# Two products of a chunked delta-rule attention as 32x32 array tiles

## The chip, the core and the metric

The kernel runs on one core of one Trainium2 chip. The metric is device time in microseconds (us), from the start to the end of one execution. Two executions of the kernel before took 905.57 and 912.49 us; their median is 909.03 us.

The core's engines run their own queues in order: TensorE (PE in the rows; its weight loads are PEld), VectorE (DVE), ScalarE (ACT), GpSimd (POOL) and SyncE (SP), which issues most transfers.

## The reference

Attention first: for each of 4 sequences and 8 heads a 48x48 state is carried over 768 positions.

```
k_n = k / (norm(k) + 1e-6)
for t in range(S):
    y[t] = q[t] @ state
    v_old = k_n[t] @ state
    state += beta[t] * outer(k_n[t], v[t] - v_old)
```

The outputs, 3072 rows of 384, go to a mixture of 8 experts: each row takes the expert with the largest of `x @ w_gate`, is multiplied by two weight matrices (384x1024, a ReLU, 1024x384), and is scaled by its softmax weight. All is fp32.

## The kernel before

The 768 positions are cut into 24 chunks of 32. One step of the main loop treats one chunk for all 4 sequences at once: partition 32b + i is position i of sequence b, so a 128-row tile holds the four sequences one below the other. "Step c" below is one turn of this loop.

Ahead of a step, `scores(c + 7)` multiplies keys by keys and queries of a chunk into `pa` (L164). ScalarE copies the key part out as `gr` (L173), and VectorE multiplies the query part by a mask that keeps only what lies within one sequence and in causal order: `qk` (L175). `gr` is stored to memory. Every fourth step `solve` loads the four chunks' key products and inverts 128 triangular 32x32 systems in place on VectorE: L249, then 30 pairs of a product (L255) and an addition (L259), then L262. The result is stored, and `fetch_step` loads it as four 32x32 blocks for each head onto the diagonal of a 128x128 tile `ub`, whose other places are zero since the start.

`chain(c)` is the step itself, in this order of dependence:
- `ph` (L291): keys times states, 16 matmuls that load 32 columns each and write to the 32 partitions of one sequence. VectorE takes it from the values: the residual `R` (L296).
- the first part of `pq` (L303): queries times states, of the same shape as `ph`.
- `pz` (L310): the triangular block times the residual, 8 matmuls, one for each head, with all 128x128 of `ub` as weights. ScalarE copies it out as `Z` (L315).
- `pw` (L323): keys times Z, in two halves of 8 matmuls, two sequences each, written to two PSUM banks. VectorE adds it to `states` (L331). The next step's `ph` needs them.
- the second part of `pq` (L335): masked scores times Z, 8 matmuls, one for each head, added onto the first part. ScalarE copies the output out as `xg` (L445).

After every fourth step `route` computes the gate of the last chunks on PE (transposes L349, products L353, counts L389 and L390) and VectorE. `pa` and `pw` share two PSUM buffers (pool `psS`); `ph`, `pq`, `pz` and the routing's tiles share four (pool `psC`). The order of the instructions on each engine is made once, when the program is built, by a scheduler that has its own idea of how long each takes; at run time each queue is worked off in that order. After the 24 steps come the experts (L508 to L555), whose weights are loaded by SP.

Of the kernel before, what the change touches and what calls it, by code (L numbers as in the profile page):

```python
# [19 lines left out]
B, H, S, D = 4, 8, 768, 48  # L20
C = 32
# [43 lines left out]
def kernel(  # L65
# [12 lines left out]
    nc = tc.nc  # L78
# [202 lines left out]
    def chain(c):  # L281
        kq, ub, kt, vt, qk = kqs.pop(c), ubufs[c % NU], kts.pop(c), vts.pop(c), qks.pop(c)
        vtl = vt[:].rearrange("p h d -> p (h d)")
        if c == 0:
            Rv = vtl
        else:
            ph = psC.tile([128, 512], FP32, name="ph", tag="pc")
            for p in range(NP):
                for b in range(B):
                    r = slice(C * b, C * b + C)  # L290
                    nc.tensor.matmul(  # L291
                        ph[r, 96 * p : 96 * p + 96], lhsT=kq[:, p, 0, r],
                        rhs=states[:, b, p, :], start=True, stop=True, skip_group_check=True,
                    )
            R = work.tile([128, DM], FP32, name="R")
            nc.vector.tensor_tensor(out=R[:], in0=vtl, in1=ph[:, 0:DM], op=OP.subtract)  # L296
            Rv = R[:]
        pq = psC.tile([128, 512], FP32, name="pq", tag="pc")
        if c > 0:
            for p in range(NP):  # L300
                for b in range(B):
                    r = slice(C * b, C * b + C)
                    nc.tensor.matmul(  # L303
                        pq[r, 96 * p : 96 * p + 96], lhsT=kq[:, p, 1, r],
                        rhs=states[:, b, p, :],
                        start=(p == 0), stop=False, skip_group_check=True,
                    )
        pz = psC.tile([128, 512], FP32, name="pz", tag="pc")
        for h in range(H):
            nc.tensor.matmul(  # L310
                pz[:, D * h : D * h + D], lhsT=ub[:, h, :], rhs=Rv[:, D * h : D * h + D],
                start=True, stop=True,
            )
        Z = work.tile([128, DM], FP32, name="Z")
        nc.scalar.activation(out=Z[:], in_=pz[:, 0:DM], func=AF.Copy)  # L315
        if c < NS - 1:
            for half in range(2):
                pw = psS.tile([128, 2, 512], FP32, name="pw", tag="ps")
                for p in range(NP):
                    for bb in range(2):  # L320
                        b = 2 * half + bb
                        r = slice(C * b, C * b + C)
                        nc.tensor.matmul(  # L323
                            pw[:, bb, 96 * p : 96 * p + 96], lhsT=kt[r, p, :],
                            rhs=Z[r, 96 * p : 96 * p + 96], start=True, stop=True,
                        )
                pv = pw[:, :, 0:DM].rearrange("q b (p w) -> q b p w", p=NP)
                for e in range(2):
                    r = slice(64 * e, 64 * e + 64)
                    sv = states[r, 2 * half : 2 * half + 2, :, D * e : D * e + D]  # L330
                    nc.vector.tensor_tensor(  # L331
                        out=sv, in0=sv, in1=pv[r, :, :, D * e : D * e + D], op=OP.add
                    )
        for h in range(H):
            nc.tensor.matmul(  # L335
                pq[:, D * h : D * h + D], lhsT=qk[:, h, :], rhs=Z[:, D * h : D * h + D],
                start=(c == 0), stop=True, skip_group_check=True,
            )
        return pq


# [93 lines left out]
    for c in range(NS):  # L435
        load_kq(c + AHEAD + 1)
        scores(c + AHEAD)
        if (c + AHEAD) % GS == GS - 1:
            solve((c + AHEAD) // GS)
            factors((c + AHEAD) // GS + 1)  # L440
        pq = chain(c)
        ss = first[c]
        if c == ss[0]:
            xg = work.tile([128, GS, ROW], FP32, name="xg")
        nc.scalar.activation(out=xg[:, c - ss[0], 0:DM], in_=pq[:, 0:DM], func=AF.Copy)  # L445
        if c in batch:
            route(ss, xg)
        fetch_step(c + 3)
        if c == NS // 2:
            weights[0] = load_w(moe_w1[0], moe_w2[0], wpool)  # L450
# [196 lines left out]
```

## Time and profile before

| | us |
|---|---|
| median of two runs | 909.03 |
| the profiled execution | 910.19 |
| its span, first to last instruction | 908.4 |
| first product of the main loop | 77.81 |
| end of the main loop's part (last routing) | 548.3 |
| experts | 579.9 to 908.4 |

| engine | busy us | share of the span |
|---|---|---|
| PE matmuls | 720.9 | 79% |
| PE weight loads | 526.7 | 58% |
| DVE | 328.1 | 36% |
| ACT | 109.5 | 12% |
| POOL | 158.1 | 17% |

Matmuls are pipelined, so a busy PE is not a PE at its peak, and weight loads overlap with matmuls. The mean granted clock of TensorE is 0.732 of full speed (0.5 is 1.2 GHz, 1.0 is 2.4 GHz).

### The profile page before, as it was taken

To read this page: it belongs to the slowest core of one execution; us is meant where nothing else is said; L and a number is where in the kernel's file an instruction comes from. 1 tells how busy PE (TensorE), PEld (TensorE's weight loads), DVE (VectorE), ACT (ScalarE), POOL (GpSimd) and SP (SyncE) were. 2 spreads that over 40 slices of the span, in tenths; PEclk is the share of its full clock that TensorE was granted. 3 is DMA by queue.
4 is the path that set the end of the run, shared out by engine and by line. 5 is a ranking of instruction groups with operands and counts; after the bars stand their busy time and mean duration, and the time that the engine had idled before them with its cause. 6 is when DMAs were issued, how large, how long until landed. Compare 5 with 4: busy or idle time off the path is not lost. (4 is left out here: it accounts for less than half of the span.)

```text
span 908.4 us, 11550 instructions
## 1 busy us (share of the span) xinstructions
PE 720.9 (79%) x4596; PEld 526.7 (58%) x4597; DVE 328.1 (36%) x897; ACT 109.5 (12%) x199; POOL 158.1 (17%) x133
## 2 busy tenths in 40 slices
PE   4515768879978897599874980399999999999993
PEld 3315658768866786488864970155555555555551
DVE  4592882395458529632552121011011111102100
ACT  2210111201110111011000110001010010101100
POOL 5201211020211112101001011303031231312101
PEclk8655767565655665567555555599999999999997
DMA  8536335631634287335112005501233432323000
GB/s 319 163 78 172 81 90 130 149 92 43 177 98 110 59 182 224 91 97 87 37 56 63 1 27 175 163 0 55 85 104 112 143 121 87 114 95 96 28 8 18
DMA packets 112345, 91.55 MB, mean 101 GB/s; under 512 B 85238, under 2 KB 96678, under 8 KB 112288
## 3 DMA queue, kind: packets, MB, share of 16 engines
q1 hardware_dynamic: 106704, 80.37, 31.7%
q0 software_dynamic: 4608, 9.47, 3.4%
q10 hardware_dynamic: 976, 0.94, 0.4%
q8 instruction: 37, 0.61, 0.3%
q14 instruction: 20, 0.16, 0.1%
HBM read 70.96 MB, written 21.36 MB: 102 GB/s over the span
## 5 line engine op out<-in xcount | busy, mean ns | idle before, releaser
L517 PE MATMUL phe<-xTe,w1t 128*128 128x448 f32 x384 | 148.4, 547 | 0.0
L533 PE MATMUL pye<-w2t,hT 128*128 128x384 f32 x384 | 125.1, 486 | 0.0
L517 PEld LDWEIGHTS phe<-xTe,w1t 128*128 128x128 f32 x384 | 73.1, 192 | 70.1 <-issue 68.2
L164 PE MATMUL pa<-kq 64*128 64x256 f32 x384 | 82.0, 593 | 33.6 <-issue 11.3
L533 PEld LDWEIGHTS pye<-w2t,hT 128*128 128x128 f32 x384 | 73.0, 190 | 51.7 <-issue 3.0
L323 PE MATMUL pw<-Z,kt 32*128 32x96 f32 x736 | 64.4, 366 | 29.5 <-issue 10.1
L164 PEld LDWEIGHTS pa<-kq 64*128 64x128 f32 x384 | 58.0, 302 | 50.0 <-issue 29.3
L310 PE MATMUL pz<-R,ub 128*128 128x48 f32 x368 | 67.5, 356 | 23.4 <-DMA ub<-solved 15.4
L335 PE MATMUL pq<-Z,qk 128*128 128x48 f32 x384 | 78.4, 383 | 6.3 <-ACT Z L315 5.7
L310 PEld LDWEIGHTS pz<-R,ub 128*128 128x128 f32 x368 | 64.3, 271 | 30.0 <-issue 17.0
L323 PEld LDWEIGHTS pw<-Z,kt 32*128 32x128 f32 x736 | 58.2, 265 | 39.9 <-issue 32.7
L335 PEld LDWEIGHTS pq<-Z,qk 128*128 128x128 f32 x384 | 74.5, 297 | 10.3 <-ACT Z L315 8.0
L331 DVE TENSOR_TENSOR states<-states,pw 64x384 f32<-64x384 f32 x92 | 50.7, 552 | 69.6 <-PE pw L323 67.7
L175 DVE TENSOR_TENSOR qk<-pa,cf 128x256 f32<-128x256 f32 x96 | 37.9, 418 | 103.9 <-ACT gr L173 101.9
L255 DVE TENSOR_TENSOR tmp<-u 128x30 f32<-128x30 f32 (+9 forms) x180 | 70.1, 389 | 4.7
L259 DVE TENSOR_TENSOR u<-u,tmp 128x30 f32<-128x30 f32 (+9 forms) x180 | 64.9, 360 | 4.2
L522 DVE TENSOR_SCALAR hT<-phe 128x448 f32<-128x448 f32 x32 | 20.0, 625 | 127.5 <-PE phe L517 127.5
L405 POOL DMA_INDIRECT lists<-ids,ri x24 | 23.9, 996 | 216.8 <-DVE ri L403 89.7
L497 POOL DMA_INDIRECT out_dram<-y,rows x24 | 24.0, 1002 | 211.5 <-ACT y L542 178.1
L291 PE MATMUL ph<-states,kq 128*32 128x96 f32 x736 | 40.6, 361 | 10.2 <-DVE states L331 10.2
L512 DVE COPY xTe<-px 128x448 f32<-128x448 f32 x24 | 14.1, 614 | 89.8 <-PE px L508 89.8
L508 PE MATMUL px<-ident,xin 128*128 128x128 f32 (+1 forms) x96 | 19.0, 303 | 33.7 <-issue 31.6
(87 smaller groups left out, 578.4 us busy)
## 6 DMA issues: line engine op xcount, KB each, us to landing
kq<-in_kq_t_dram SPq DMA_DIRECT2D x24, 512.0 KB
w1t<-in_moe_w_dram SPq DMA_DIRECT2D x8, 1536.0 KB
w2t<-in_moe_w_dram SPq DMA_DIRECT2D x8, 1536.0 KB
kt<-in_k_tok_dram SPq DMA_DIRECT2D x24, 256.0 KB
kb<-in_k_blk_dram SPq DMA_DIRECT2D x6, 768.0 KB
vb<-in_v_blk_dram SPq DMA_DIRECT2D x6, 768.0 KB
sv<-vb SPq DMA_DIRECT2D x6, 768.0 KB
vt<-sv SPq DMA_DIRECT2D x96, 48.0 KB
```

What stands on the lines that cost most here:

```text
L164: nc.tensor.matmul(pa[:, e, pp, :], lhsT=kq[r, 2 * g + pp, 0, :], rhs=kq[r, 2 * g + pp, :, :].rearrange("p j w -> p (j w)"), start=True, s ...
L175: nc.vector.tensor_tensor(out=heads(qk)[:, e], in0=pa[:, e, :, 128:256], in1=blockmask.unsqueeze(1).to_broadcast([128, 2, 128]), op=OP.mult,)
L255: nc.vector.tensor_tensor(out=tv, in0=u[:, 0:j, j].unsqueeze(2).to_broadcast([128, j, w]), in1=u[:, j, j + 1 : C].unsqueeze(1).to_broadcas ...
L259: nc.vector.tensor_tensor(out=u[:, 0:j, j + 1 : C], in0=u[:, 0:j, j + 1 : C], in1=tv, op=OP.add)
L291: nc.tensor.matmul(ph[r, 96 * p : 96 * p + 96], lhsT=kq[:, p, 0, r], rhs=states[:, b, p, :], start=True, stop=True, skip_group_check=True,)
L310: nc.tensor.matmul(pz[:, D * h : D * h + D], lhsT=ub[:, h, :], rhs=Rv[:, D * h : D * h + D], start=True, stop=True,)
L323: nc.tensor.matmul(pw[:, bb, 96 * p : 96 * p + 96], lhsT=kt[r, p, :], rhs=Z[r, 96 * p : 96 * p + 96], start=True, stop=True,)
L331: nc.vector.tensor_tensor(out=sv, in0=sv, in1=pv[r, :, :, D * e : D * e + D], op=OP.add)
L335: nc.tensor.matmul(pq[:, D * h : D * h + D], lhsT=qk[:, h, :], rhs=Z[:, D * h : D * h + D], start=(c == 0), stop=True, skip_group_check=True,)
L497: nc.gpsimd.indirect_dma_start(out=out, out_offset=bass.IndirectOffsetOnAxis(ap=index, axis=0), in_=y[0:w, :], in_offset=None, bounds_chec ...
L517: nc.tensor.matmul(ph[:], lhsT=w1t[:, s, f * 128 : f * 128 + 128], rhs=xT[:, s, :], start=(s == 0), stop=(s == NK - 1),)
L533: nc.tensor.matmul(py[:], lhsT=hT[:, f, t * 128 : t * 128 + w], rhs=w2t[:, f, :], start=(f == 0), stop=(f == NF - 1),)
```

## The change

Both products are issued as 4 matmuls for each head in place of one: each takes one sequence's 32x32 diagonal block as weights and writes to that sequence's 32 partitions. The sums are the same, since the other blocks are zero. The tiles themselves, the zeros around the blocks and the mask are unchanged. The lines below move by two (`pw` from L323 to L325) and then four (`pq` from L335 to L339).

```diff
         for h in range(H):
-            nc.tensor.matmul(
-                pz[:, D * h : D * h + D], lhsT=ub[:, h, :], rhs=Rv[:, D * h : D * h + D],
-                start=True, stop=True,
-            )
+            for b in range(B):
+                r = slice(C * b, C * b + C)
+                nc.tensor.matmul(
+                    pz[r, D * h : D * h + D], lhsT=ub[r, h, r], rhs=Rv[r, D * h : D * h + D],
+                    start=True, stop=True, skip_group_check=True,
+                )
...
         for h in range(H):
-            nc.tensor.matmul(
-                pq[:, D * h : D * h + D], lhsT=qk[:, h, :], rhs=Z[:, D * h : D * h + D],
-                start=(c == 0), stop=True, skip_group_check=True,
-            )
+            for b in range(B):
+                r = slice(C * b, C * b + C)
+                nc.tensor.matmul(
+                    pq[r, D * h : D * h + D], lhsT=qk[r, h, r], rhs=Z[r, D * h : D * h + D],
+                    start=(c == 0), stop=True, skip_group_check=True,
+                )
```

The scheduler orders the program anew. On PE in step 4, from `pz` to the next step's `pz` (the number after `ub_` is a buffer, x32 a count of matmuls), it stood so before:

```order
L310 MATMUL pz<-R,ub_95 128x48 x8
L335 MATMUL pq<-Z,qk 128x48 x8
L164 MATMUL pa<-kq 128x256 x8
L323 MATMUL pw<-Z,kt 128x96 x16
L291 MATMUL ph<-states,kq 32x96 x2
L303 MATMUL pq<-states,kq 32x96 x2
L291 MATMUL ph<-states,kq 32x96 x14
L303 MATMUL pq<-states,kq 32x96 x14
L310 MATMUL pz<-R,ub_97 128x48 x8
```

And so after the change:

```order
L312 MATMUL pz<-R,ub_95 32x48 x32
L164 MATMUL pa<-kq 128x256 x8
L325 MATMUL pw<-Z,kt 128x96 x8
L339 MATMUL pq<-Z,qk 32x48 x5
L325 MATMUL pw<-Z,kt 128x96 x8
L339 MATMUL pq<-Z,qk 32x48 x27
L291 MATMUL ph<-states,kq 32x96 x2
L303 MATMUL pq<-states,kq 32x96
L291 MATMUL ph<-states,kq 32x96 x14
L303 MATMUL pq<-states,kq 32x96 x15
L312 MATMUL pz<-R,ub_97 32x48 x32
```

The second part of `pq` moved from ahead of the scores to behind the first half of `pw`; in steps 7, 11 and 16 it also moved behind `pw` or into it, and `pa` of steps 8 and 12 moved from ahead of `pz` to behind it.

On DVE the residual `R` of step 7 stood before in the midst of the solve of the third group, 26 rows ahead of L262:

```order
L331 TENSOR_TENSOR states<-states,pw 64x8x48
L255 TENSOR_TENSOR tmp<-u 128x228
L259 TENSOR_TENSOR u<-u,tmp 128x12x19
L255 TENSOR_TENSOR tmp<-u 128x220
L296 TENSOR_TENSOR R<-vt,ph 128x384
L259 TENSOR_TENSOR u<-u,tmp 128x11x20
L255 TENSOR_TENSOR tmp<-u 128x210
L259 TENSOR_TENSOR u<-u,tmp 128x10x21
L255 TENSOR_TENSOR tmp<-u 128x198
```

After the change the whole solve stands ahead of it, and the masks of chunk 14 too:

```order
L255 TENSOR_TENSOR tmp<-u 128x84
L259 TENSOR_TENSOR u<-u,tmp 128x3x28
L255 TENSOR_TENSOR tmp<-u 128x58
L259 TENSOR_TENSOR u<-u,tmp 128x2x29
L255 TENSOR_TENSOR tmp<-u 128x30
L259 TENSOR_TENSOR u<-u,tmp 128x30
L262 TENSOR_TENSOR u<-u,fout 128x1024
L175 TENSOR_TENSOR qk<-pa,cf 128x2x128 x4
L296 TENSOR_TENSOR R<-vt,ph 128x384
L333 TENSOR_TENSOR states<-states,pw 64x8x48 x4
```

What moved: the solve now stands between the residuals of steps 6 and 7 with no state update in its first 45 rows; the group of steps 8 to 11 changed likewise, and the group of steps 12 to 15 had this order already.

## Rows read from the trace of the kernel before

**Rows 1.** The page: busy time of PE, and granted clock in 40 slices.
```profile
PE 720.9 (79%) x4596; PEld 526.7 (58%) x4597; DVE 328.1 (36%) x897; ACT 109.5 (12%) x199; POOL 158.1 (17%) x133
...
PEclk8655767565655665567555555599999999999997
```

**Rows 2.** Windows: stretch, length, busy us of each engine, granted clock, DMA share, GB/s.
```profile
77.80:148.40 70.60, 55.68 (x576) 49.75 (x580) 44.59 (x123) 10.87 (x20) 9.02 (x4) 0.69 0.43 114
148.40:167.50 19.10, 18.09 (x160) 15.88 (x154) 5.30 (x16) 2.18 (x4) 4.08 (x4) 0.50 0.59 89
167.50:236.20 68.70, 57.93 (x474) 50.05 (x470) 41.79 (x120) 9.98 (x18) 8.97 (x4) 0.57 0.39 111
236.20:248.90 12.70, 12.12 (x175) 10.93 (x168) 5.27 (x16) 2.18 (x4) 2.95 (x3) 0.77 0.75 186
248.90:317.90 69.00, 56.19 (x456) 48.91 (x454) 42.13 (x119) 9.88 (x18) 9.94 (x5) 0.60 0.33 91
317.90:330.00 12.10, 11.52 (x162) 10.39 (x158) 5.35 (x17) 2.18 (x4) 1.98 (x2) 0.78 0.82 186
330.00:406.10 76.10, 56.73 (x472) 50.18 (x467) 42.73 (x120) 9.88 (x18) 10.90 (x6) 0.54 0.51 137
406.10:488.80 82.70, 59.89 (x600) 55.32 (x592) 37.01 (x116) 7.32 (x15) 7.38 (x8) 0.58 0.32 70
488.80:548.30 59.50, 53.71 (x460) 50.25 (x460) 12.41 (x44) 6.33 (x14) 6.43 (x6) 0.53 0.07 19
579.90:908.40 328.50, 312.02 (x992) 165.76 (x992) 42.27 (x72) 35.53 (x64) 69.25 (x68) 0.97 0.24 77
```

**Rows 3.** Timeline of step 14: start us, us, engine, line, operation, [idle before].
```profile
355.04 0.56 DVE L296 TENSOR_TENSOR R<-vt,ph 128x384 f32<-128x384 f32 x1
...
374.99 1.23 DVE L262 TENSOR_TENSOR u<-u,fout 128x1024 f32<-128x1024 f32 x1
...
376.98 3.00 PE L323 MATMUL pw<-Z,kt 32*128 32x96 f32 x32 [8.29 <-issue]
...
382.93 0.55 DVE L296 TENSOR_TENSOR R<-vt,ph 128x384 f32<-128x384 f32 x1 [1.60 <-PE ph L291]
```

**Rows 4.** Timeline of PE: first and last product of steps 20 to 22.
```profile
488.83 3.62 PE L310 MATMUL pz<-R,ub 128*128 128x48 f32 x16 [15.43 <-DMA ub<-solved]
...
522.95 3.65 PE L335 MATMUL pq<-Z,qk 128*128 128x48 f32 x16
```

**Rows 5.** Groups by line: busy us, mean ns of one, idle before and its releaser.
```profile
L335 PE MATMUL pq<-Z,qk 128*128 128x48 f32 x384 | 78.4, 383 | 6.3 <-ACT Z L315 5.7 <-issue 0.6
L310 PE MATMUL pz<-R,ub 128*128 128x48 f32 x368 | 67.5, 356 | 23.4 <-DMA ub<-solved 15.4 <-DVE R L296 7.9
```

**Rows 6.** Timeline of PE: the first product, then steps 1 and 4.
```profile
77.81 3.62 PE L310 MATMUL pz<-vt,ub 128*128 128x48 f32 x16 [22.71 <-DMA ub<-solved]
...
91.65 0.87 PE L291 MATMUL ph<-states,kq 128*32 128x96 f32 x32
92.34 0.84 PE L303 MATMUL pq<-states,kq 128*32 128x96 f32 x32
93.67 1.99 PE L310 MATMUL pz<-R,ub 128*128 128x48 f32 x16 [0.49 <-DVE R L296]
...
146.84 1.51 PE L291 MATMUL ph<-states,kq 128*32 128x96 f32 x32
148.13 1.51 PE L303 MATMUL pq<-states,kq 128*32 128x96 f32 x32
149.56 3.65 PE L310 MATMUL pz<-R,ub 128*128 128x48 f32 x16
...
157.37 3.79 PE L164 MATMUL pa<-kq 64*128 64x256 f32 x16
```

**Rows 7.** Windows in those two passages of ph and pq, columns as in rows 2.
```profile
91.70:93.20 1.50, 1.48 (x66) 1.26 (x64) 1.17 (x5) 1.43 (x2) 0.00 (x0) 1.00 0.17 26
146.90:149.60 2.70, 2.70 (x66) 2.42 (x65) 1.74 (x10) 0.00 (x0) 0.00 (x0) 0.50 0.98 311
```

## The prediction

> **What bounds the kernel now.** I read the page's shares first, then the span cut into stretches, then the TensorE timeline, then the waits inside one group of steps. "Step c" is one turn of the loop over 24 chunks; a "product" is one of the two that change: the triangular block times the residual (pz) and the masked scores times Z (the last writes of pq). TensorE (PE) is the busiest engine, but at 79% of the span it is not simply full, and the row of granted clocks moves between 5 and 8 (tenths) until the experts begin [rows 1]. The cut into stretches shows where a change of these products can act [rows 2]: the experts' part, from 579.9 us on, has none of them and keeps its 328.5 us. Before 77.8 us no product has run. Only the 470 us from 77.8 to 548.3 can move, and what follows moves along with their end.
>
> Inside them three kinds of stretch stand side by side. From 488.8 to 548.3 PE is busy 53.7 of 59.5 us and VectorE (DVE) 12.4: here PE is the bound, at a clock of 0.53, that is nearly all at 1.2 GHz. In the stretches cut at 148.4, 236.2 and 317.9 PE has 95% too. In the longer ones (167.5, 248.9, 330.0) PE is idle for 11 to 19 us and DVE busy for 42: the in-place triangular solve of the next group of four steps runs there, and PE waits for state updates that stand in DVE's queue behind it. The sharpest example is step 14 [rows 3]: R, the residual, at 355.04, the solve ends at 374.99 + 1.23, and only then pw begins, after 8.29 us of idle PE. The last link is the transfer of the solved blocks: pz of step 20 waited 15.43 us for ub [rows 4].
>
> **The price of one product.** The two groups are 67.5 us for 23 steps and 78.4 us for 24 [rows 5]; the first step adds 3.6 [rows 6], together 149.5 us for 48 products. Each fp32 matmul is two passes, so a product has 16 passes now and 64 after. 29 of the 48 take 3.6 us or more (the first at 77.81, the last at 522.95 [rows 4, 6]), 7 take 1.99 as at 93.67 [rows 6], and 12 lie between, at 2.5 in the mean. The cold form is 15 gaps and a last pass of 0.41 us: (3.65 - 0.41)/15 = 216 ns a gap. These gaps are weight loads: 128 columns are loaded for only 48 that stream.
>
> After the change every pass loads 32 columns and streams 48, in four array tiles in turn. No row shows that shape. The nearest are ph and the first part of pq, which load 32 columns and stream 96, also in four tiles in turn. From 146.84 to 148.13 their 32 passes start 40.3 ns apart, from 91.65 to 92.34 only 21.6 ns [rows 6]; the granted clock is 0.50 there (1.2 GHz) and 1.00 here (2.4 GHz) [rows 7]. So the ends are 21.6 ns (the fastest pace that the trace has) and 40.3 ns (streaming not cheaper although it is half as long): 63 gaps and a last pass of 0.37 make 1.7 to 2.9 us. I take 28 ns, nearer to the half of 40.3 than to the whole, because the halved streaming should count until some pace of issue limits it: 63 x 0.028 + 0.37 = 2.15 us, **1.5 us less than a cold product**. For a warm one 21.6 to 27 ns give 1.6 to 2.0 us against 1.99; I take 1.7, and 1.9 for those between. The trace's floor of 21.6 ns is below what the Trainium skill states ("TensorE: Matmul & The Clock Gate", section "Wait — 56ns, not 53.3ns?"): matmuls never start less than about 25 ns apart. By that figure the low end would be 63 x 0.025 + 0.37 = 1.95 us; the row at 91.65 disagrees with it.
>
> In all PE is spared 149.5 - (29 x 2.15 + 7 x 1.7 + 12 x 1.9) = 52 us. 48 x 48 = 2,304 more passes and as many weight loads are issued; at 91.65 the queue gave out 32 of each in 0.69 us, so I put no extra cost on issue. Nothing is taken off DVE, ScalarE or the transfers: the zeros around ub's blocks and the mask stay.
>
> **What reaches the end.** I go through the stretches of [rows 2].
> - 77.8 to 148.4 (70.6 us). The cold pz and pq of step 0 stand ahead of the scores that release the next solve: -3.0. Then DVE is the limit; step 3's warm pair -0.6.
> - 148.4 to 167.5 (19.1). One cold pair: -3.0.
> - 167.5 to 236.2 (68.7). Here the order changes: DVE now runs the whole solve between R of step 6 and R of step 7, where before it was spread up to step 7's end. That is the pattern of step 14 [rows 3], where R to R took 382.93 - 355.04 = 27.9 us and the pair of products lay hidden under the solve. For step 6: 27.9, less 3.7 for the last solve rows that now stand behind the masks, plus 3.8 for the scores of chunk 14 that PE now does ahead of step 7's residual (pa [rows 6]): 28.0. Step 5 I put at 18.5 and step 7 with its routing at 22.5. Sum 69.0: +0.3. The cold products of step 7 are gained and spent again on the wait in step 6.
> - 236.2 to 248.9: a warm and a middling product, -1.2. 248.9 to 317.9 (69.0): the same new order, 69.0, no change.
> - 317.9 to 330.0: -1.1. 330.0 to 406.1 (76.1): this one already has the step 14 pattern, so it keeps its order: step 13's cold pair -3.0, step 14's hidden, step 15's -1.1.
> - 406.1 to 488.8 (82.7): steps 16 and 17 before the last solve: 0.6 + 0.4 + 0.3 + 1.5; pz of step 18 1.5; step 19's pair, ahead of the routing that DVE waits for, 3.0: -7.3. The wait for ub at 488.83 moves with the solve; it stays.
> - 488.8 to 548.3: six cold products and two between, all on PE's path: -10.1. What is late next in a step is pw and the state updates, which still fit under the shorter pq (DVE is busy 12.4 us of the 59.5).
>
> Sum: -3.0 - 0.6 - 3.0 + 0.3 - 1.2 - 1.1 - 4.1 - 7.3 - 10.1 = -30 us of the 52. The profiled execution took 910.19 us (span 908.4), 1.2 above the median of 909.03: 880 in the one, 879 in the other; **I forecast 880 us**. About 20 cold products pass through; at the price of 1.7 that is 9 us better (871), at 2.9 15 us worse, and the middling ones give up 3 more (898).
>
> **Rivals.**
> 1. *The four tiles don't run at once* (slower). Four row tiles now write one PSUM bank, pz or pq, each in its own 32 partitions. In the trace row tiles do overlap: pa's 16 passes of 256 columns take 3.79 us [rows 6], half of what they would one after another at 96 columns in 4 x 40.3 ns. And column tiles overlap in ph. But no row has several row tiles in one bank. One at a time, a pass of 48 columns would be 80 ns cold: 63 x 0.08 + 0.4 = 5.4 us, 1.8 more than now; with 20 cold products and the warm ones about +45: 955 us. It decides above 3.24/63 = 51 ns a pass. Chance 0.10. The Trainium skill speaks for it: "TensorEngine Tiling (Array Packing)", section "Restrictions and Gotchas", says that row tiles write to different banks and cannot use one bank at the same time. No row here has that case; these tiles differ in their columns as well.
> 2. *The new order eats the gain* (no change). If steps 6 and 10 show an idle time like step 14's 8.29 us on top of my reckoning, 16.6 us go: 897 us. For it speaks that PE's idle time is largest where the solve is bundled (the stretch from 330.0 in [rows 2]); against it that the solve then ends earlier. Chance 0.15.
> 3. *The clock rises* with the denser passes: the 0.50 of the cold stretches gets nearer the 0.77 of 236.2 to 248.9 [rows 2]. Three steps in the last stretch would each lose some 4 us, and the rest as much again: 855 us. Chance 0.09.
> 4. *The clock falls.* Each stretch of [rows 2] ran 2 x (clock - 0.5) of its length at 2.4 GHz, 87 us in all between 77.8 and 548.3; at 1.2 GHz throughout, with half of it on the path, +45: 925 us. What went before the rises (ph with pq, pa) is unchanged, which speaks against it. Chance 0.06.
>
> **How the numbers follow.** My forecast has 0.60, its own range is 871 to 898, and 0.12 of it lies above 890.8. About 2% (18 us) can be told from no change: faster is below 890.8, slower above 927.2. Faster: 0.48 + 0.09 = 0.57. Same: 0.12 + 0.15 + half of rival 4, 0.03 = 0.30. Slower: 0.10 + 0.03 = 0.13. The range runs from 860 to 908; left out are rivals 1 and 4 and the lower part of rival 3, together 0.20.
>
> **What would show it.** In the profile after: the pz and pq groups near 48 x 2.0 us in sum; the stretch of steps 20 to 23 near 49 us; steps 6 and 10 with one long idle time of PE ahead of pw; the wait for ub of step 20 still there; the 31.6 us between the last step and the experts, and the experts' 328.5 us, as they were. I am wrong if a product takes over 3 us with the clock at 0.5, if the clock of 488.8 to 548.3 is no longer near 0.5, or if the stretches from step 5 to step 8 and 9 to 12 are longer than 72 us.

## The result, and the profile after

The changed kernel took 832.78 us (832.73 and 832.82) against 909.03 (905.57 to 912.49): a ratio of 0.916, with a 95% interval from 0.901 to 0.931. It is faster, as forecast, but by 76 us where 29 were forecast, and outside the range of 860 to 908. In a later comparison it came to 838.95 us, a ratio of 0.931 (0.921 to 0.940). Medians below are of all executions of a kernel, while a ratio and its interval leave out those over 1.5% above the kernel's fastest, so a ratio can differ a little from the quotient of two medians.

The page of the changed kernel answers to [rows 1]; its profiled execution took 832.73 us, with a span of 831.0.

```profile
PE 597.4 (72%) x6900; PEld 404.3 (49%) x6901; DVE 329.8 (40%) x897; ACT 109.2 (13%) x199; POOL 158.4 (19%) x133
...
PEclk9665857776865785588558556999999999999997
```

PE has 2,304 more matmuls and 123.5 us less busy time, and the granted clock over the span is 0.802 where it was 0.732. DVE, ScalarE and GpSimd are as busy as before.

The groups by line (busy us, mean ns of one | idle before, its releasers) answer to [rows 5]:

```profile
L164 PE MATMUL pa<-kq 64*128 64x256 f32 x384 | 77.6, 567 | 67.7 <-DMA kq<-in_kq_t_dram 44.3 <-issue 10.2 <-ACT gr L173 6.1
L325 PE MATMUL pw<-Z,kt 32*128 32x96 f32 x736 | 55.2, 327 | 32.9 <-issue 18.0 <-DVE qk L175 6.6 <-ACT Z L317 4.6
...
L339 PE MATMUL pq<-Z,qk 32*32 32x48 f32 x1536 | 27.1, 221 | 6.4 <-ACT Z L317 6.1 <-issue 0.2
L312 PE MATMUL pz<-R,ub 32*32 32x48 f32 x1472 | 27.0, 228 | 26.6 <-DMA ub<-solved 15.5 <-issue 7.2 <-DVE R L296 3.8
...
L312 PE MATMUL pz<-vt,ub 32*32 32x48 f32 x64 | 2.0, 276 | 22.5 <-DMA ub<-solved 22.5
```

The two products cost 27.1 + 27.0 + 2.0 = 56.1 us instead of 149.5: 93.4 less, where the forecast had 52. Two of the groups that the change doesn't touch had, before:

```profile
L164 PE MATMUL pa<-kq 64*128 64x256 f32 x384 | 82.0, 593 | 33.6 <-issue 11.3 <-DMA kq<-in_kq_t_dram 10.6 <-ACT gr L173 5.3
...
L323 PE MATMUL pw<-Z,kt 32*128 32x96 f32 x736 | 64.4, 366 | 29.5 <-issue 10.1 <-DVE u L259 7.8 <-DVE qk L175 6.2
```

So two other things stand in the rows of the change. `pw` fell from 64.4 to 55.2 us; with `pa` (82.0 to 77.6), `ph` (40.6 to 36.6), the first part of `pq` (44.4 to 35.6) and the routing's matmuls (46.1 to 34.9) that is 37.6 us off work that is the same, matmul for matmul. And `pa` now waits 44.3 us for its keys and queries (`kq`); before it waited 10.6.

Single products on the timeline of PE (start us, us, ... [idle before]) answer to [rows 6]:

```profile
77.62 1.97 PE L312 MATMUL pz<-vt,ub 32*32 32x48 f32 x64 [22.52 <-DMA ub<-solved]
...
141.81 1.50 PE L312 MATMUL pz<-R,ub 32*32 32x48 f32 x64
...
172.28 0.88 PE L339 MATMUL pq<-Z,qk 32*32 32x48 f32 x64 [0.68 <-ACT Z L317]
```

The common slow form is 1.50 us (the granted clock is 0.50 from 141.81 to 143.30): a last pass of 0.28 (the mean of the first step's, cold, in the group above) leaves (1.50 - 0.28)/63 = 19.4 ns a pass. The fast form of 0.88 (1.00 from 172.28 to 173.16) has about 10 ns. The first product of the loop is the dearest, 1.97 us.

The windows (length, busy us of PE, PEld, DVE, ACT and POOL, granted clock, DMA share, GB/s) are cut at the first `ph` of steps 4, 8, 12 and 16 and at the first `pz` of steps 0 and 20:

```profile
77.60:139.10 61.50, 41.96 (x922) 35.12 (x922) 43.83 (x119) 10.87 (x20) 9.01 (x4) 0.69 0.49 119
139.10:213.80 74.70, 48.47 (x1001) 40.40 (x1000) 48.03 (x135) 12.13 (x22) 13.08 (x8) 0.73 0.50 130
213.80:287.60 73.80, 49.40 (x1001) 41.00 (x1000) 47.93 (x135) 12.13 (x22) 12.93 (x8) 0.71 0.49 127
287.60:366.10 78.50, 46.80 (x1001) 39.50 (x1000) 48.56 (x135) 12.06 (x22) 12.93 (x8) 0.70 0.60 159
366.10:432.80 66.70, 41.68 (x1018) 36.68 (x1018) 37.61 (x120) 7.22 (x15) 7.56 (x7) 0.68 0.42 88
432.80:470.40 37.60, 30.14 (x844) 26.65 (x844) 12.41 (x45) 6.12 (x14) 5.99 (x6) 0.73 0.13 34
501.80:831.00 329.20, 312.42 (x992) 166.01 (x992) 42.25 (x72) 35.52 (x64) 69.07 (x68) 0.97 0.24 76
```

The kernel before, cut at the same places (its sixth stretch, from 488.80, is in [rows 2]):

```profile
77.80:146.80 69.00, 54.08 (x536) 48.19 (x536) 43.92 (x119) 10.87 (x20) 9.02 (x4) 0.70 0.42 110
146.80:234.60 87.80, 76.02 (x620) 65.88 (x619) 47.05 (x135) 12.16 (x22) 13.04 (x8) 0.56 0.43 106
234.60:316.30 81.70, 68.31 (x617) 59.88 (x616) 47.44 (x135) 12.05 (x22) 12.89 (x8) 0.63 0.40 111
316.30:404.50 88.20, 68.25 (x617) 60.56 (x616) 48.04 (x134) 12.05 (x22) 12.88 (x8) 0.58 0.55 144
404.50:488.80 84.30, 61.49 (x633) 56.91 (x632) 37.71 (x121) 7.32 (x15) 7.38 (x8) 0.58 0.32 70
```

So the gains are 7.5, 13.1, 7.9, 9.7, 17.6 and 21.9 us; the gap ahead of the experts (31.4 us) and the experts (329.2) are as before. In the five later stretches the clock rose by 0.08 to 0.20. Steps 20 to 23, on the timeline of PE, show best what that means:

```profile
432.78 0.33 PE L312 MATMUL pz<-R,ub 32*32 32x48 f32 x2 [15.15 <-DMA ub<-solved]
...
443.03 1.23 PE L312 MATMUL pz<-R,ub 32*32 32x48 f32 x64
444.88 1.67 PE L325 MATMUL pw<-Z,kt 32*128 32x96 f32 x32 [0.62 <-ACT Z L317]
446.48 0.88 PE L339 MATMUL pq<-Z,qk 32*32 32x48 f32 x64
...
449.93 0.88 PE L312 MATMUL pz<-R,ub 32*32 32x48 f32 x64
```

The wait for `ub` is where it was, 15.15 us. Behind it the products of steps 21 and 22 take 1.23 and then 0.88, where the same stretch of before still had 3.65 at 522.95 [rows 4], and `pw` takes 1.67 (a slow one takes 3.00 [rows 3]).

The new order shows in step 6, on the timeline of all engines (SPq is SyncE's queue of transfers):

```profile
170.10 0.56 DVE L296 TENSOR_TENSOR R<-vt,ph 128x384 f32<-128x384 f32 x1
...
172.03 2.79 POOL L231 TENSOR_TENSOR vb<-vb,norm 128x1536 f32<-128x1536 f32 x1 [10.45 <-DVE norm L219]
...
174.85 0.34 SPq L234 DMA_DIRECT2D sv<-vb  x1
...
175.71 0.91 SPq L150 DMA_DIRECT2D kq<-in_kq_t_dram  x1
...
181.17 3.58 PE L164 MATMUL pa<-kq 64*128 64x256 f32 x16 [8.01 <-DMA kq<-in_kq_t_dram]
...
191.46 3.55 PE L325 MATMUL pw<-Z,kt 32*128 32x96 f32 x32 [6.71 <-issue]
...
198.13 1.23 DVE L262 TENSOR_TENSOR u<-u,fout 128x1024 f32<-128x1024 f32 x1
...
202.16 0.54 DVE L296 TENSOR_TENSOR R<-vt,ph 128x384 f32<-128x384 f32 x1
```

From R to R are 32.06 us with the whole solve between. PE is idle twice in it: 8.01 us for `kq`, whose load stands on SyncE behind the store of the scaled values (L234), which waits for GpSimd's product, and 6.71 us ahead of `pw`. Step 10 has 7.54 and 6.47, step 14 has 16.16 and 3.54.

### The profile page after: what moved, and what is told of

It is laid out like the page before. It is cut to its first block, busy times and chain, and to the rows that moved or that the text cites. A ratio compares the mean times of both kernels' runs of the same rounds, so it can differ in the third digit from the quotient of the medians.

```text
span 831.0 us, 16145 instructions
## 1 busy us (share of the span) xinstructions
PE 597.4 (72%) x6900; PEld 404.3 (49%) x6901; DVE 329.8 (40%) x897; ACT 109.2 (13%) x199; POOL 158.4 (19%) x133
## 5 line engine op out<-in xcount | busy, mean ns | idle before, releaser
L164 PE MATMUL pa<-kq 64*128 64x256 f32 x384 | 77.6, 567 | 67.7 <-DMA kq<-in_kq_t_dram 44.3
L325 PE MATMUL pw<-Z,kt 32*128 32x96 f32 x736 | 55.2, 327 | 32.9 <-issue 18.0
L255 DVE TENSOR_TENSOR tmp<-u 128x30 f32<-128x30 f32 (+9 forms) x180 | 75.0, 417 | 4.6
L325 PEld LDWEIGHTS pw<-Z,kt 32*128 32x128 f32 x736 | 49.8, 229 | 42.2 <-issue 29.4
L259 DVE TENSOR_TENSOR u<-u,tmp 128x30 f32<-128x30 f32 (+9 forms) x180 | 61.0, 339 | 4.3
L291 PE MATMUL ph<-states,kq 128*32 128x96 f32 x736 | 36.6, 329 | 15.3 <-DVE states L333 15.0
L173 ACT ACTIVATE gr<-pa 128x512 f32<-128x512 f32 x48 | 28.3, 596 | 143.9 <-PE pa L164 113.6
L312 PE MATMUL pz<-R,ub 32*32 32x48 f32 x1472 | 27.0, 228 | 26.6 <-DMA ub<-solved 15.5
L512 PE MATMUL px<-ident,xin 128*128 128x128 f32 (+1 forms) x96 | 18.9, 303 | 33.6 <-issue 31.5
L312 PEld LDWEIGHTS pz<-R,ub 32*32 32x32 f32 x1472 | 22.8, 124 | 32.7 <-issue 23.7
L530 ACT ACTIVATE hT<-phe 128x448 f32<-128x448 f32 x32 | 17.4, 544 | 153.8 <-PE phe L521 153.8
```

What stands on the lines that cost most here:

```text
L164: nc.tensor.matmul(pa[:, e, pp, :], lhsT=kq[r, 2 * g + pp, 0, :], rhs=kq[r, 2 * g + pp, :, :].rearrange("p j w -> p (j w)"), start=True, s ...
L173: nc.scalar.activation(out=heads(gr), in_=pa[:, :, :, 0:128], func=AF.Copy, scale=-1.0)
L255: nc.vector.tensor_tensor(out=tv, in0=u[:, 0:j, j].unsqueeze(2).to_broadcast([128, j, w]), in1=u[:, j, j + 1 : C].unsqueeze(1).to_broadcas ...
L259: nc.vector.tensor_tensor(out=u[:, 0:j, j + 1 : C], in0=u[:, 0:j, j + 1 : C], in1=tv, op=OP.add)
L291: nc.tensor.matmul(ph[r, 96 * p : 96 * p + 96], lhsT=kq[:, p, 0, r], rhs=states[:, b, p, :], start=True, stop=True, skip_group_check=True,)
L312: nc.tensor.matmul(pz[r, D * h : D * h + D], lhsT=ub[r, h, r], rhs=Rv[r, D * h : D * h + D], start=True, stop=True, skip_group_check=True,)
```

## The experiments

Each kernel ran beside the kernel before on the same chip. "Theory" in the expectations is my explanation at that time; none of these forms leaves out a part of the computation.

**Each product alone.** `pz_only` is the change with the 128x128 loop kept for `pq`, `pq_only` with it kept for `pz`:

```diff
 # pz_only, against the change
-            for b in range(B):
-                r = slice(C * b, C * b + C)
-                nc.tensor.matmul(pq[r, ...], lhsT=qk[r, h, r], rhs=Z[r, ...], ...)
+            nc.tensor.matmul(pq[:, ...], lhsT=qk[:, h, :], rhs=Z[:, ...], ...)
```

> Only pz is issued as 32x32 tiles; the masked product stays 128x128, and the order of the queues is that of the kernel before. Theory (a pass costs its stream shared by four tiles, 20 ns at 1.2 GHz and 10 ns at 2.4; the thinner products also let the clock rise): the pz groups fall from 71 us to 26 to 36, the mean granted clock from 0.732 to 0.75 or more, the time to 865 to 885 us. Rival (the new order of the changed kernel brought much of its gain): here that order is missing, and the time stays above 890.

> Only the masked product is issued as 32x32 tiles; pz stays 128x128, the order is that of the kernel before. Theory: its group falls from 78 us to 27 to 40, the time to 870 to 890 us (less than pz alone, since it is off the path in the steps where pw comes first). If both halves together save more than the 76 us of the whole change, the new order or new waits took the difference; if less, the clock gained from both being thin.

Measured: `pz_only` 846.79 us (831.91 to 851.03), `pq_only` 850.43 (845.54 to 853.53; ratio 0.939, 0.932 to 0.945), before 905.1. Each gave more than expected, and the two gains, 58.3 and 54.7 us, add up to 113, not to 76. The groups by line of `pq_only`:

```profile
L164 PE MATMUL pa<-kq 64*128 64x256 f32 x384 | 74.6, 549 | 35.0 <-DMA kq<-in_kq_t_dram 12.2 <-issue 10.4 <-ACT gr L173 6.2
L310 PE MATMUL pz<-R,ub 128*128 128x48 f32 x368 | 63.0, 340 | 25.4 <-DMA ub<-solved 15.2 <-DVE R L296 10.1
```

`pz`, here in its old form, has become cheaper (63.0 against 67.5), and so has `pa` (74.6 against 82.0): one cheap product already lifts the clock, to 0.781 (0.786 in `pz_only`), and the second only to 0.802. So part of what each half gains is the same rise of the clock, had once and not twice. Besides, both halves keep the old pattern on DVE, and `pa` waits 12.2 us for `kq` in `pq_only` and 18.1 in `pz_only`, not 44: the whole change may pay something that neither half pays. These runs don't show how the difference divides.

**Which way of cutting.** `cols` cuts the weights in columns only; `outer` puts the loop over sequences outside the one over heads, so that one array tile works at a time. Both have the change's order on DVE.

```diff
 # cols, against the change
-                    pz[r, ...], lhsT=ub[r, h, r], rhs=Rv[r, ...],
+                    pz[r, ...], lhsT=ub[:, h, r], rhs=Rv[:, ...],
 # outer, against the change
-        for h in range(H):
-            for b in range(B):
+        for b in range(B):
+            for h in range(H):
```

> Both products as tiles of 128 rows and 32 columns: each matmul takes all 128 rows of the tile (three quarters of them zeros) and writes one sequence's 32 partitions; as many instructions as the change, and its order. Theory (four column tiles at once are what counts): pz and pq passes at 20 and 10 ns as in the change, product groups 52 to 62 us, time 825 to 840 us. Rival (the cut in rows counts too): passes of 30 ns or more at 1.2 GHz, groups over 80 us, time over 850.

> The 32x32 tiles of the change, with the loop over sequences outside the loop over heads: 16 passes in a row use the same tile, so that at most one tile has work at a time. Order otherwise that of the change. Theory (overlap of four tiles is what makes a pass cheap): 80 ns a pass at 1.2 GHz and 40 at 2.4, a product 5.2 or 2.7 us, product groups 150 us or more, time 930 to 990 us. Rival (only the shorter weight load counts): passes of 20 to 54 ns, time 833 to 880.

Measured: `cols` 830.22 us (823.83 to 833.85; ratio 0.915, 0.908 to 0.922), with 27.5 and 28.0 us for the two products: cutting the rows as well adds nothing. `outer` 941.61 us (937.95 to 944.37; ratio 1.040, 1.033 to 1.046). Its groups by line, and a slow product on its timeline:

```profile
L339 PE MATMUL pq<-Z,qk 32*32 32x48 f32 x1536 | 98.4, 263 | 5.6 <-ACT Z L317 5.6
...
L312 PE MATMUL pz<-R,ub 32*32 32x48 f32 x1472 | 77.3, 236 | 16.6 <-DMA ub<-solved 14.2 <-DVE R L296 2.3
```

```profile
159.22 4.41 PE L312 MATMUL pz<-R,ub 32*32 32x48 f32 x64
```

(4.41 - 0.28)/63 = 65.5 ns a pass at a granted clock of 0.50 (80 were expected), where the change has 19.4: the same matmuls in another order cost over three times as much. What makes the change's product cheap is that four tiles in turn run at once, not that a tile is small.

**Larger tiles.** `t64` has two 64x64 tiles for each head, each with two sequences:

```diff
-            for b in range(B):
-                r = slice(C * b, C * b + C)
+            for b in range(2):
+                r = slice(2 * C * b, 2 * C * b + 2 * C)
```

> Both products as 64x64 tiles, two sequences in each: 16 matmuls for a product, two tiles in turn, and the order of the queues is that of the kernel before, not that of the change. Theory on the price: a pass is bounded by the load of 64 columns, shared by two tiles, 53 ns at 1.2 GHz and 27 at 2.4, a product 2.0 or 1.1 us, the product groups 65 to 80 us in sum. Theory on the order (the new order and its waits for kq ate some 15 us of the change's gain): with these dearer products the time is still 815 to 833 us and the waits of pa for kq are under 25 us. Rival (the new order costs nothing): 840 to 860.

Measured: 818.37 us (811.59 to 820.49; ratio 0.909, 0.899 to 0.919). It ran once more, beside the change on one chip:

> The changed kernel as it is, beside t64 and the other two on one chip, so that the differences between them carry no chip with them. Both theories: 830 to 834 us.

> 64x64 tiles once more, which keep the old order on VectorE (residuals of steps 6, 7, 10 and 11 inside the solve). Theory (the new order costs the change 14 us or more): again at least 10 us under the changed kernel. Rival (the 14 us were the chip's): within 5 us of it.

Measured there: the change 838.95 us (836.53 to 845.24; 830 to 834 were expected), `t64` 818.94 (818.36 to 820.48; ratio to before 0.907, 0.899 to 0.914). It beats the change by 20.0 us although its products are dearer, as its groups by line show (the change in that comparison had 30.2 + 29.2 + 2.0 us):

```profile
L164 PE MATMUL pa<-kq 64*128 64x256 f32 x384 | 70.6, 524 | 41.1 <-DMA kq<-in_kq_t_dram 21.4 <-issue 10.8 <-ACT gr L173 5.5
...
L312 PE MATMUL pz<-R,ub 64*64 64x48 f32 x736 | 34.4, 252 | 23.8 <-DMA ub<-solved 14.2 <-DVE R L296 9.5
L339 PE MATMUL pq<-Z,qk 64*64 64x48 f32 x768 | 33.2, 242 | 8.0 <-ACT Z L317 7.4 <-issue 0.6
L312 PE MATMUL pz<-vt,ub 64*64 64x48 f32 x32 | 2.3, 304 | 22.4 <-DMA ub<-solved 22.4
```

With half as many matmuls the scheduler keeps the old order on DVE. The timelines of PE, of `t64` and then of the change on that chip, in steps 6 and 7:

```profile
175.36 2.02 PE L312 MATMUL pz<-R,ub 64*64 64x48 f32 x32 [1.42 <-DVE R L296]
...
191.82 1.95 PE L312 MATMUL pz<-R,ub 64*64 64x48 f32 x32
```

```profile
171.31 0.94 PE L312 MATMUL pz<-R,ub 32*32 32x48 f32 x64
...
203.35 0.88 PE L312 MATMUL pz<-R,ub 32*32 32x48 f32 x64 [0.26 <-DVE R L296]
```

16.5 us against 32.0; part of it comes back, since in `t64` the solve's rows lie in steps 4, 5 and 7, but from step 4's `pz` to step 12's `t64` needs 138.6 us and the change 147.3. From there to step 16 both have the same pattern on DVE, and `t64` still gains 5.4 us (72.3 against 77.7), with a shorter wait for `kq` in step 14 (5.95 against 15.05). From step 16's `pz` to the experts it gains 4.6 more (134.8 against 139.5). So 8.7 us of the lead, not all of it, lie in the steps where the two orders on DVE differ; the mean clock over them is 0.70 in both.

**The loads.** `kqearly` is the change with the loads of `kq` two steps earlier, `t64_early` the same for `t64`; `svq` and `t64_svq` issue the store L234 from GpSimd's queue, off SyncE.

```diff
 # kqearly
-            kqs[c] = stage.tile([128, NP, 2, 128], FP32, name="kq")
+            kqs[c] = stage.tile([128, NP, 2, 128], FP32, name="kq", bufs=11)
-        load_kq(c + AHEAD + 1)
+        load_kq(c + AHEAD + 3)
 # svq
-        nc.sync.dma_start(out=scaled[g], in_=vb[:].rearrange("p t d -> p (t d)"))
+        nc.gpsimd.dma_start(out=scaled[g], in_=vb[:].rearrange("p t d -> p (t d)"))
```

> The change, with the loads of kq issued two steps earlier (11 buffers in place of 9); the scheduler then also orders the steps anew. Theory (the 44 us in which pa waits for kq are on the path): those waits fall under 10 us and the time falls to 790 to 815 us. Rival (behind pa stands the wait for the masks, which VectorE makes only after the solve): the wait moves to pw, and the time stays at 825 to 840 us.

> 64x64 tiles and the earlier loads of kq together; the order is nearly that of the kernel with the early loads. If the price of a product is what counts in that order, it is 5 to 15 us slower than 32x32 tiles with early loads; if VectorE's solve is the bound there, the two are within 5 us of each other.

> 32x32 tiles as in the change; the store of the scaled values (L234) is issued by GpSimd instead of SyncE, so that it no longer holds up the scores' loads behind it. The scheduler's order moves with it: the solve of the second and third group of steps is spread over the residuals again (as before the change), that of the fourth is still one piece. Theory (the change lost time to the order and to loads late on SyncE): pa waits under 25 us for kq in all (44 in the change), and 10 to 20 us come off: 812 to 822 us. Rival (the wait only moves, as with the earlier loads): pz waits that much longer for R and ub, 828 to 834 us.

> 64x64 tiles and the store L234 on GpSimd; the solve is spread over the residuals in all groups but the last. Theory: pa waits under 15 us for kq (22 in t64) and 3 to 8 us come off t64: 810 to 815 us. Rival: the wait moves to R and ub, 817 to 825 us.

Measured: `kqearly` 828.46 us (823.64 to 834.27; ratio 0.918, 0.906 to 0.930, the change's own 0.916), `t64_early` 844.8 (837.59 to 849.55), 26 more than `t64` beside it and 16 more than `kqearly`, where 5 to 15 were the price expected of the dearer products. The wait moved, as the groups by line of `kqearly` show:

```profile
L164 PE MATMUL pa<-kq 64*128 64x256 f32 x384 | 80.4, 573 | 36.4 <-issue 10.2 <-ACT gr L173 7.8 <-DMA kq<-in_kq_t_dram 5.4
...
L312 PE MATMUL pz<-R,ub 32*32 32x48 f32 x1472 | 30.5, 238 | 74.7 <-DVE R L296 37.2 <-DMA ub<-solved 36.6 <-issue 0.7
```

`svq` took 830.95 us (822.03 to 837.02), 8 under the change beside it. Three of its four executions (822.03 to 833.04) lie below all of the change's (836.53 to 845.24); the fourth, the profiled one, took 837.02, and the intervals of the ratios overlap (0.905 to 0.927 and 0.921 to 0.940). In that profile the wait for `kq` is down to 5.7 us, but `pw` waits 31.5 with the label "issue" (16.8 in the change). The two longest of them, in steps 10 and 14 on the timeline of PE:

```profile
254.62 3.91 PE L325 MATMUL pw<-Z,kt 32*128 32x96 f32 x32 [11.19 <-issue]
...
343.03 3.00 PE L325 MATMUL pw<-Z,kt 32*128 32x96 f32 x32 [16.95 <-issue]
```

`t64_svq` took 817.93 us (815.54 to 819.3), 1.0 under `t64`: there the shorter wait for `kq` (6.7 against 21.4) bought nothing. So in these forms late loads are hardly a cost of their own: where the loads came sooner, PE waited elsewhere, for the residual, for `ub` or ahead of `pw`. Whether `svq` gained a little stays open.

**The clock alone.** `wide` and its kin are the kernel before, with its 128x128 products. Only each matmul of `pz` streams more columns, into places that the next head's matmul writes over:

```diff
 # wide88, against the kernel before; 64, 112 and 128 likewise
-                pz[:, D * h : D * h + D], lhsT=ub[:, h, :], rhs=Rv[:, D * h : D * h + D],
+                pz[:, D * h : min(DM, D * h + 88)], lhsT=ub[:, h, :],
+                rhs=Rv[:, D * h : min(DM, D * h + 88)],
```

> The kernel before, with 128x128 products, but each matmul of pz streams up to 128 columns of the residual in place of 48; what it writes beyond its own 48 is overwritten by the next head. The loads of 128 columns already take 216 ns a pass at 1.2 GHz, and 128 columns stream in about as long, so a product of pz should take 3.7 to 3.9 us cold as before, with the array streaming all the time. Theory (the clock follows how much of the time TensorE streams): the mean granted clock rises from 0.74 to 0.76 or more and the time falls to 880 or below. Rival (the clock rose because cheaper products bring the dense stretches together in time): clock 0.73 to 0.75, time 900 to 915.

> The kernel before (128x128 products, its order on VectorE) with each matmul of pz streaming up to 64 columns of the residual in place of 48; the columns behind the 48 are written over by the next head's. Theory (TensorE's clock follows how much it streams, and the gain of the 128-column form came from it): a cold pz stays at 3.6 us, clock 0.73 to 0.76, 890 to 905 us. Rival (the 128-column form gained by the scheduler's new order): no change, 900 to 912 us, clock 0.73 to 0.74.

> The same with up to 88 columns. Theory: between 64 and 128 columns, 872 to 893 us, clock 0.75 to 0.79. Rival: no change, 900 to 912 us.

> The same with up to 112 columns, the widest that keeps the order of the kernel before. Theory: close to the 128-column form (865 us), 860 to 878 us, clock 0.78 to 0.81. Rival: no change, 900 to 912 us.

| columns of `pz` | us, median (range) | ratio to before (95%) | clock |
|---|---|---|---|
| 48 (before, beside the next three) | 908.16 (901.36 to 917.23) | 1 | 0.732 in the profile of before |
| 64 | 898.46 (891.52 to 904.43) | 0.987 (0.977 to 0.997) | 0.742 |
| 88 | 861.45 (855.49 to 876.91) | 0.947 (0.936 to 0.958) | 0.792 |
| 112 | 863.3 (857.67 to 871.13) | 0.949 (0.938 to 0.959) | 0.793 |
| 128 (beside a before of 909.65) | 865.45 (862.17 to 869.08) | 0.962 (0.950 to 0.974) | 0.801 |

With 88 columns the time came out below the 872 to 893 us that were expected; the other three lie in their ranges.

The forms with 64, 88 and 112 columns keep the old pattern of solve and residuals on DVE. On PE the order with 64 columns is the old one too, but for single matmuls. With 88 it moved in three places: in step 4 the second part of `pq` went into and behind the first half of `pw`, and in steps 7 and 11 `pa` and half of `pw` went ahead of some of the routing's matmuls. From `pz` to `pz` these three steps gained 20.0 of the 50.9 us by which the two profiles differ between the first product and the experts, and there the order may have a share. The other 21 steps, in nearly the old order, gained 30.9 us. From step 20 to the experts the order is the very same on both engines; the window of before, and then that of `wide88`:

```profile
488.83:579.90 91.07, 53.76 (x461) 50.27 (x461) 13.81 (x54) 6.33 (x14) 9.99 (x10) 0.52 0.28 87
```

```profile
446.39:528.90 82.51, 45.61 (x460) 42.48 (x461) 13.79 (x54) 6.21 (x14) 9.28 (x9) 0.58 0.30 96
```

That is 8.6 us less, with 0.58 granted in place of 0.52 and no instruction moved.

Groups by line of `wide88`, and two of its products on the timeline of PE:

```profile
L336 PE MATMUL pq<-Z,qk 128*128 128x48 f32 x384 | 62.7, 326 | 6.9 <-ACT Z L316 6.9
L324 PE MATMUL pw<-Z,kt 32*128 32x96 f32 x736 | 55.4, 325 | 33.3 <-DVE u L259 9.0 <-issue 8.4 <-DVE qk L175 7.4
```

```profile
446.39 3.62 PE L310 MATMUL pz<-R,ub 128*128 128x88 f32 x16 [17.46 <-DMA ub<-solved]
...
459.83 1.99 PE L310 MATMUL pz<-R,ub 128*128 128x88 f32 x16
```

The slow product with 88 columns (clock 0.50) takes the 3.62 us that it took with 48 [rows 4], and the fast one (clock 1.00) the 1.99 [rows 6]: the wider stream fits under the weight loads and makes nothing cheaper at a given clock. Yet `pq`, of which nothing changed, falls from 78.4 to 62.7 us and `pw` from 64.4 to 55.4, since more of them are in their fast form. So the clock brought most of the 46.7 us between the medians: by the count of steps about 31 of 51, and some part of the other 20.

## Why the prediction was wrong

**The bound** held: all of the gain lies between 77.6 and 470.4 us, and the gap and the experts kept their times.

**The price of a pass failed, at its low end.** The sentence was that the ends are 21.6 ns, the fastest pace that the trace has, and 40.3. A slow product runs at 19.4 ns a pass, below that end. 21.6 ns was the pace of passes of 96 columns at 2.4 GHz; for half the columns it was no floor. At either clock the price is half of that of 96 columns: 19.4 against 40.3 and about 10 against 21.6. The streaming of four tiles at once sets the pace, and no limit of issue shows. A slow product costs 1.50 us and not 2.15, a fast one 0.88 and not 1.7. With the forecast's own count (29 slow, 7 fast, 12 between, now at 1.2) the sum would have been 149.5 - (29 x 1.50 + 7 x 0.88 + 12 x 1.2) = 85 us spared and not 52. That the trace already disagreed with the floor of about 25 ns in the Trainium skill ("TensorE: Matmul & The Clock Gate", section "Wait — 56ns, not 53.3ns?") was right; these passes, in tiles that run at once, go still further below it.

**The sum failed by holding the clock.** A faster clock was rival 3, with a chance of 0.09, priced for 855 us as another case; the forecast let the granted clock stand "nearly all at 1.2 GHz" in the last stretch. It is 0.73 there now, the sign that was named as the one that would prove me wrong. The argument under rival 4, that `ph`, `pq` and `pa` ahead of the rises are unchanged, was no ground for a steady clock: the products themselves are part of what PE does before it rises. `wide88` shows it: with products at the old price, more streaming under the same weight loads raised the clock, and the steps that nearly kept their order gained 30.9 us. In the change the 37.6 us are off work whose slow and fast forms are as long as before (`pw` 3.00 and 1.67), so I put them to the clock, and it makes the products 85 + 8 = 93 us cheaper.

Together the two errors come to about the miss. The forecast let 30 of 52 spared us reach the end, 0.58. At that share 33 us more from the price give 19, and 37.6 + 8 from the clock 26: 880 - 19 - 26 = 835 us. The split is an estimate and not measured, and it stands on the clock being lifted by the change as a whole. The share fits: 123.5 us less busy time of PE brought 76, which is 0.62.

**Stretch by stretch.** Every one gained more than its term: 7.5 against 3.6 in the first; 21.9 against 10.1 in the last, where PE's busy time fell by 53.7 - 30.1 = 23.6 us and nearly all of it reached the end, as that term had it.

**The new order** was the step that came out best. Steps 6 and 10 do show the idle time of PE ahead of `pw` that I named. From R to R step 6 takes 32.06 us against the 28.0 of the sum; what I missed is the late `kq`, at 8.01 us. Rival 2 had 8.29 us for each such step on top; half of that came. Still these steps gained (13.1 us in the second stretch), by the clock and by products that are cheaper in steps 4, 5 and 7. That the order has a price is shown by `t64`: with dearer products and at like clocks it needs 8.7 us less in the steps where the orders on DVE differ. How its whole lead of 20 us divides into the solve's place, the loads and the clock (0.807 against 0.793) stays open: no run has the change's tiles with all of the old order, and `svq`, which comes nearest, is not clear of the change.

**Rival 1** fell. Four row tiles write one bank, each in its own partitions and columns of the array, and run at once: `outer`, where they can't, needs 65.5 ns a pass, and 941.61 us came out (rival 1 had 80 ns and 955). What the Trainium skill says for this rival ("TensorEngine Tiling (Array Packing)", section "Restrictions and Gotchas": different row tiles cannot access one PSUM bank at the same time) did not show for tiles that also differ in their columns.

## What to carry to other kernels

When PE's time is to be cut, read the granted clock of the stretch first and ask how much PE will stream there after the edit: the clock is part of the price of every other matmul there, and here, by the estimate above, it was worth half as much as the cheaper passes themselves. Products whose weight loads are longer than their streams can be cut into tiles that run in turn (64x64 did it best here), or can stream more columns for nothing, as `wide88` did. And look at the order that the scheduler makes of the edit: the one that came with 32x32 tiles may have cost more than these tiles bring over 64x64.

## What was not expected of the hardware

- A matmul that streams 40 columns more, all of them thrown away, made a kernel 5.3% faster (4.2 to 6.4): the product's own 3.62 us stayed, and the granted clock went from 0.73 to 0.79. Some 20 of its 51 us lie in three steps where the order on PE moved as well.
- The gain isn't in proportion to the columns: 64 gave 1.3%, and 88, 112 and 128 between 3.8 and 5.3. How much of this step is the order on PE, which moved with 88 columns and not with 64, was not tested.
- At 1.2 GHz 64 passes of 48 columns took 1.50 us with four tiles in turn and 4.41 with one tile at a time: 3.4 times the pace a pass (65.5 against 19.4 ns), not 4.
